# A new head and new plan values for a fused softmax-attention and linear-attention kernel

## The chip, the cores and the metric

One Trainium2 chip, one core. The metric is the device time of one execution in microseconds (us). A run's *span*, from the profiler, is about 2 us shorter than its time. Every run also reports the mean clock granted to TensorE (1.00 is full speed).

## The reference

Two attention branches work on the same x (2048 tokens, width 512, 32 heads of 16) and are mixed by a gate.

```python
g = sigmoid((x * gate_w).sum(-1, keepdims=True))
a = softmax(q k^T / 4) v  -> heads joined -> @ A_wo        # branch A, q, k, v = x @ A_wqkv
b = phi(q) (phi(k)^T v) / (phi(q) sum(phi(k)))  -> @ B_wo  # branch B, phi = [softmax(u), softmax(-u)], u = q @ w_phi
out = g * a + (1 - g) * b
```

The expensive part is branch A: 32 heads x 2048 x 2048 scores need an exponential each.

## The kernel before

The kernel is a generator. Python code declares operations (engine, assumed duration, dependencies, priority), a list scheduler simulates the five engines once, and each engine's instructions are then emitted in the order that the simulation found. On the chip the order is fixed; semaphores only make an engine wait. Tables of numbers ("plan values") steer the scheduler.

```python
GROUPS = (3, 2)          # score tiles per exponential, in turn
LEAD = [16.455..., ...]  # when work is released, against its deadline
PACE = [2.41..., 0.458...]
OFF, PRI, SHY, FILL, SLIP, POLY, SHAPE = ...   # 33 numbers each: one per block of heads
DVE_COUNT = (1, 3, 2, ...)   # key tiles per block whose exponential VectorE computes (sum 79)
```

Branch A works in 32 blocks of 16 key tiles x 4 head pairs. Most score tiles (1732 of 128 x 512) go TensorE -> PSUM ring of 5 banks -> ScalarE exponential -> a ring of 15 SBUF slots (`ET`) -> TensorE product with V. The other 316 score tiles get their exponential from a polynomial on VectorE and GpSimd (`EW`, `Ef`, `Em`, `ED`). Branch B and the output projection fill the gaps. TensorE also runs matmuls with zeros (dummies) to keep its clock up.

The head, as it was (cut):

```python
# loads: x tiles on SyncE, three weight slices on ScalarE's queue
self.d_xr = [dma("sp", ... xr[:, t, :] <- x tile t ...) for t in range(4)]
self.d_wq = [dma("act", wpart(0, P), ...)]
self.d_wk = [dma("act", wpart(D, P), ...)]
self.d_wv = [dma("act", wpart(2 * D, P), ...)]

# transposes of x on TensorE; a dummy (ps_ring <- iden, zero) ahead and after each tile
for k in range(WARM + 5):                 # WARM = 3
    if k < WARM or k > WARM:
        ... dummy matmul 128x512 ...
    t = k - WARM
    if 0 <= t < 4:
        ... 4 transposes of x tile t; after tiles 1 and 3 copies to xT ...

# Q of 512 tokens: project, cast to qst, four masked copies qT[:, n, i] = qst * par[:, n, i]
# K of 512 tokens: project, one ScalarE copy to kT; then the first score matmuls
self.o_kT[(cp, j)] = s.op("act", 0.47, ... kT[:, cp, 0:QCH] <- bank ...)
```

An exponential waits for its scores, and for the `ET` slots it overwrites, which the product with V must have read:

```python
deps = [o_qk]
if ub - NSLOT >= 0:
    deps.append(self.o_pv[(ub - NSLOT) // 4])
```

The softmax here doesn't subtract the row's maximum and nothing guards it: scores larger than these inputs give would overflow.

## Time and profile before

| | before |
|---|---|
| time | 835.79 us (3 runs, 835.7 to 837.38) |
| span of the profiled run | 833.6 us |
| first exponential starts | 10.76 us |
| stream of exponentials | 10.76 to 826.06 us: 815.30 us |
| tail after the last exponential | 7.53 us |

The page of the kernel before: busy time by engine, then the chain of work that ended last, by engine and by line, then the costliest group (busy us, mean ns | idle just before).

```profile
PE 765.5 (92%) x5815; PEld 226.2 (27%) x5898; DVE 792.3 (95%) x1157; ACT 819.4 (98%) x765; POOL 298.1 (36%) x399
...
ACT 96%; PE 2%; DVE 1%; DMA 0%; SPq 0%; issue 0%
ACT ET L867 92%; ACT phi L1121 4%; PE ps_ring L849 1%; DMA xr<-in_A_x_dram 0%; DVE EW L952 0%; PE ps_ring L1189 0%; PE ps_mp L1189 0%; PE ps_ot L895 0%; PE ps_mp L709 0%; SPq L626 0%; DVE wphi L1049 0%; PE ps_ot L983 0%; ACT outz L1230 0%; ACT kT L756 0%; ACT xT L693 0%
...
L867 ACT ACTIVATE ET<-ps_ring 128x1536 bf16<-128x1536 f32 (+1 forms) x693 | 791.2, 1340 | 1.3 <-PE ps_ring L849 0.9
```

ScalarE (ACT) is busy 98% of the span, and 96% of the chain is ScalarE. VectorE and TensorE are nearly as busy, so they have little slack.

A record's duration includes more than ScalarE's throughput: neighbouring records overlap. The Trainium skill, "Perfetto Trace Analysis", section "DVE / Act Engine Instruction (TENSOR_ADD, Activation, etc)", explains it: a record ends when the write is acknowledged, while the next instruction may start its prefetch when the previous one has finished executing. The trace agrees: here are the two shapes of the exponential (groups by shape; after the first bar the busy time in us and the mean duration in ns).

```profile
L867 ACT ACTIVATE ET<-ps_ring 128x1536 bf16<-128x1536 f32 x346 | 537.5, 1554 | 1.3 <-PE ps_ring L849 0.9 <-PE ps_ot L895 0.3
L867 ACT ACTIVATE ET<-ps_ring 128x1024 bf16<-128x1024 f32 x347 | 391.0, 1127 | 0.0
```

The records last 1.554 and 1.127 us, but the medians of the distance from one end to the next are 1.343 and 0.917 us (0.490 us for a `phi` activation). I use those three distances throughout: what a distance exceeds them by is called a **wait in the stream**, also where the profile shows no idle engine. Summed over the stream before, these waits are 0.82 us (0.44 us at 759 us, 0.31 us between 69 and 75 us). 346 x 1.343 + 347 x 0.917 + 64 x 0.490 + 0.2 (two small activations of the gate) = 814.5 us is the floor of this stream.

The head of the kernel before (timeline: start us, duration us, engine, line, operation, count, and in brackets the idle time before it and what ended it):

```profile
0.73 1.58 ACTq L620 DMA_DIRECT2D WA<-in_A_wqkv_dram  x3
...
0.74 1.81 SPq L626 DMA_DIRECT2D xr<-in_A_x_dram  x4
...
1.53 1.46 PE L674 MATMUL ps_ring<-zero,iden 128*128 128x512 bf16 x3 [1.53 <-POOL iden L656]
...
6.22 0.28 PE L681 MATMUL ps_mp<-iden,xr 128*128 128x128 bf16 x2 [0.37 <-DMA xr<-in_A_x_dram]
...
6.66 0.60 ACT L693 ACTIVATE xT<-ps_ring 128x512 bf16<-128x512 bf16 x1 [3.03 <-PE ps_ring L681]
...
7.31 1.90 PE L709 MATMUL ps_mp<-xT,WA 128*128 128x512 bf16 x8 [0.47 <-ACT xT L693]
8.38 0.69 DVE L726 CAST qst<-ps_mp 128x512 bf16<-128x512 f32 x1 [1.30 <-PE ps_mp L709]
9.11 1.14 DVE L730 TENSOR_SCALAR qT<-qst,par 128x512 bf16<-128x512 bf16 x4
...
9.25 0.60 ACT L756 ACTIVATE kT<-ps_mp 128x512 bf16<-128x512 f32 x1 [1.99 <-PE ps_mp L709]
...
10.76 2.37 ACT L867 ACTIVATE ET<-ps_ring 128x1536 bf16<-128x1536 f32 x2 [0.91 <-PE ps_ring L849]
```

The reader sees the path: x tiles issued by SyncE, the last one landed at 6.18 us (chain of waits), its transposes at 6.22, the copy to `xT` at 6.66, projections of Q and K from 7.31, the cast of Q at 8.38, masked copies at 9.11, the copy of K at 9.25, the first exponential at 10.76.

The end of ScalarE's timeline, before: the last exponential ends at 759.44 + 66.62 = 826.06 us.

```profile
759.44 66.62 ACT L867 ACTIVATE ET<-ps_ring 128x1536 bf16<-128x1536 f32 x59 [0.33 <-PE ps_ot L895]
829.02 1.27 ACT L1230 ACTIVATE outz<-ps_mp,gcol 128x512 bf16<-128x512 f32 x2 [2.96 <-PE ps_mp L1189]
```

### The profile page before, as it was taken

To read this page: it belongs to the slowest core of one execution; us is meant where nothing else is said; L and a number is where in the kernel's file an instruction comes from. 1 tells how busy PE (TensorE), PEld (TensorE's weight loads), DVE (VectorE), ACT (ScalarE), POOL (GpSimd) and SP (SyncE) were. 2 spreads that over 40 slices of the span, in tenths; PEclk is the share of its full clock that TensorE was granted. 3 is DMA by queue.
4 is the path that set the end of the run, shared out by engine and by line. 5 is a ranking of instruction groups with operands and counts; after the bars stand their busy time and mean duration, and the time that the engine had idled before them with its cause. 6 is when DMAs were issued, how large, how long until landed. Compare 5 with 4: busy or idle time off the path is not lost.

```text
span 833.6 us, 14440 instructions
## 1 busy us (share of the span) xinstructions
PE 765.5 (92%) x5815; PEld 226.2 (27%) x5898; DVE 792.3 (95%) x1157; ACT 819.4 (98%) x765; POOL 298.1 (36%) x399
## 2 busy tenths in 40 slices
PE   8899999999999999898989999989998999889998
PEld 3223333232232322222222222222222222222222
DVE  4999999999989999999999999999999999999886
ACT  6999999999999999999999999999999999999997
POOL 1244334132213432343422433442444434442523
PEclk9999999999999999999999999999999999999999
DMA  6230100000001010101210001010000001100001
GB/s 123 59 78 2 55 4 1 4 5 4 4 14 23 11 23 15 21 11 23 42 29 20 11 10 35 17 23 10 15 11 4 17 10 23 15 10 4 4 20 33
DMA packets 49123, 17.61 MB, mean 21 GB/s; under 512 B 41504, under 2 KB 49056, under 8 KB 49056
## 3 DMA queue, kind: packets, MB, share of 16 engines
q1 hardware_dynamic: 47472, 16.29, 8.5%
q8 instruction: 46, 0.75, 0.4%
q10 hardware_dynamic: 1584, 0.39, 0.2%
q14 instruction: 21, 0.17, 0.1%
HBM read 3.69 MB, written 2.10 MB: 7 GB/s over the span
## 4 chain that ended last, share of the span: by engine, by line
ACT 96%; PE 2%; DVE 1%; DMA 0%; SPq 0%; issue 0%
ACT ET L867 92%; ACT phi L1121 4%; PE ps_ring L849 1%; DMA xr<-in_A_x_dram 0%; DVE EW L952 0%; PE ps_ring L1189 0%; PE ps_mp L1189 0%; PE ps_ot L895 0%; PE ps_mp L709 0%; SPq L626 0%; DVE wphi L1049 0%; PE ps_ot L983 0%; ACT outz L1230 0%; ACT kT L756 0%; ACT xT L693 0%
## 5 line engine op out<-in xcount | busy, mean ns | idle before, releaser
L867 ACT ACTIVATE ET<-ps_ring 128x1536 bf16<-128x1536 f32 (+1 forms) x693 | 791.2, 1340 | 1.3 <-PE ps_ring L849 0.9
L849 PE MATMUL ps_ring<-qT,kT 64*128 64x512 bf16 x1732 | 343.6, 385 | 53.8 <-ACT ET L867 40.9
L966 POOL TENSOR_SCALAR ED<-EW 128x512 int16<-128x512 int16 (+1 forms) x306 | 211.5, 706 | 401.8 <-DVE Em L975 96.5
L952 DVE TENSOR_SCALAR EW<-ps_mp 128x512 int32<-128x512 f32 x316 | 204.8, 678 | 6.5 <-PE ps_mp L941 4.4
L895 PE MATMUL ps_ot<-ET,Vaug 128*17 128x512 bf16 x1732 | 168.3, 384 | 0.6 <-DVE T L1012 0.4
L849 PEld LDWEIGHTS ps_ring<-qT,kT 64*128 64x128 bf16 x1732 | 71.6, 93 | 270.4 <-ACT ET L867 244.2
L962 POOL TENSOR_SCALAR Ef<-EW 128x1024 f16<-128x1024 uint16 (+1 forms) x85 | 83.4, 981 | 121.4 <-DVE ED L977 30.3
L912 PE MATMUL ps_ot<-zero,iden 128*32 128x512 bf16 (+2 forms) x716 | 106.0, 378 | 0.3 <-issue 0.2
L941 PE MATMUL ps_mp<-qT,kT 64*128 64x512 bf16 (+1 forms) x285 | 102.0, 380 | 2.8 <-ACT phi L1121 0.8
L977 DVE TENSOR_TENSOR ED<-ED,Em 128x2048 uint16<-128x2048 int16 x79 | 99.6, 1261 | 5.1 <-POOL ED L966 4.8
L975 DVE TENSOR_TENSOR Em<-Ef,Em 128x2048 f16<-128x2048 f16 x79 | 97.7, 1237 | 0.5
L971 DVE TENSOR_TENSOR Em<-Ef 128x2048 f16<-128x2048 f16 x79 | 96.6, 1223 | 0.8 <-POOL Ef L962 0.5
L895 PEld LDWEIGHTS ps_ot<-ET,Vaug 128*17 128x17 bf16 x1732 | 41.0, 87 | 135.7 <-issue 125.1
L962 DVE TENSOR_SCALAR Ef<-EW 128x1024 f16<-128x1024 uint16 (+1 forms) x91 | 56.5, 630 | 0.1
L973 DVE TENSOR_SCALAR Em<-Em 128x2048 f16<-128x2048 f16 x79 | 55.8, 706 | 0.2
L912 PEld LDWEIGHTS ps_ot<-zero,iden 128*32 128x32 bf16 (+2 forms) x723 | 35.4, 95 | 24.0
L941 PEld LDWEIGHTS ps_mp<-qT,kT 64*128 64x128 bf16 (+1 forms) x316 | 29.1, 95 | 45.1 <-DVE EW L952 19.5
L1125 DVE TENSOR_REDUCE fsum<-phi 128x64 f32<-128x1024 bf16 x32 | 38.3, 1198 | 2.6 <-ACT phi L1121 2.6
L1127 DVE TENSOR_TENSOR phi<-phi,frec 128x1024 bf16<-128x1024 bf16 x32 | 39.8, 1247 | 0.1
L1121 ACT ACTIVATE phi<-ps_mp 128x512 bf16<-128x512 f32 x64 | 38.2, 710 | 0.0
L709 PE MATMUL ps_mp<-xT,WA 128*128 128x512 bf16 x118 | 35.9, 383 | 1.5 <-issue 0.9
L709 PE MATMUL ps_mp<-Wp,xT 128*128 128x512 bf16 x109 | 34.8, 384 | 1.0 <-issue 0.6
(83 smaller groups left out, 391.9 us busy)
## 6 DMA issues: line engine op xcount, KB each, us to landing
qT<-qst SPq DMA_DIRECT2D x120, 16.0 KB, 1.8
out_dram<-outt SPq DMA_DIRECT2D x12, 128.0 KB, 1.7
WA<-in_A_wqkv_dram SPq DMA_DIRECT2D x3, 384.0 KB, 4.8
xr<-in_A_x_dram SPq DMA_DIRECT2D x4, 128.0 KB, 3.1
WBV<-in_B_wqkv_dram SPq DMA_DIRECT2D x1, 512.0 KB, 3.9
WoA<-in_A_wo_dram SPq DMA_DIRECT2D x1, 512.0 KB, 3.7
WoB<-in_B_wo_dram SPq DMA_DIRECT2D x1, 512.0 KB, 4.5
out_dram<-outz SPq DMA_DIRECT2D x4, 128.0 KB, 1.7
```

The lines of the kernel that those rows point to most:

```text
L849: return lambda e: e.matmul(self.ps_ring[:, x % RING, :], self.kT[r, g // 2, kt * P:(kt + 1) * P], self.qT[r, n % 2, i, :], start=True, st ...
L867: self.o_exp.append(s.op("act", w * 0.434 + 0.045, lambda e, b0=b0, s0=s0, w=w: e.activation(self.ET[:, s0:s0 + w, :], self.ps_ring[:, b0: ...
L895: return lambda e: e.matmul(self.ps_ot[32 * i:32 * i + VSL, :], self.Vaug[:, kt, h, :], self.ET[:, (4 * p + k) % NSLOT, :], start=(kt == 0 ...
L912: return lambda e: e.matmul(self.ps_ot[c:c + nc, :], self.iden[r:r + nr, 0:nc], self.zero[r:r + nr, :], start=False, stop=False, tile_posi ...
L941: return lambda e: e.matmul(self.bk(b), self.kT[r, cp, kt * P:(kt + 1) * P], self.qT[r, n % 2, i, :], start=True, stop=True, tile_position ...
L952: ws.append(s.op("dve", 0.605, lambda e, i=i, b=b: e.tensor_scalar(self.EW[:, ew.idx, i * QCH:(i + 1) * QCH], self.bk(b), float(EC), float ...
L962: fs = [s.op("pool", U * 8.26e-4 + 0.28, lambda e, c=c: e.tensor_scalar(self.Ef[:, ef.idx, U * c:U * c + U], half(0, dt.uint16, c, U), flo ...
L966: hs = [s.op("pool", W * 8.26e-4 + 0.165, lambda e, c=c: e.tensor_scalar(self.ED[:, ed.idx, W * c:W * c + W].bitcast(dt.int16), half(1, dt ...
L971: u = s.op("dve", 1.13, lambda e: e.tensor_tensor(self.Em[:], Ef(), Ef(), ALU.mult), fs + [self.ed_prev], pr, frees=[ef], port=True)
L975: g_ = s.op("dve", 1.13, lambda e: e.tensor_tensor(self.Em[:], Ef(), self.Em[:], ALU.mult), [q], pr, frees=[ef], port=True)
L977: vs = [s.op("dve", 1.13, lambda e: e.tensor_tensor(out(), out().bitcast(dt.int16), self.Em[:], ALU.add), [g_] + hs, pr, port=True)]
L1121: ex.append(s.op("act", 0.478, lambda e, sg=sg: e.activation(self.phi[:, ph.idx, :, sg, :], self.bk(b).rearrange("p (h f) -> p h f", f=DH) ...
```

## The change

Its intent: start the exponentials earlier (x tiles on two queues with weights behind them; fewer dummies; only 128 tokens of K ahead of the first scores, the other 384 into a spare PSUM bank) and fit the plan values to it.

```diff
-GROUPS = (3, 2)
+GROUPS = (2, 3)
-WARM = 3
+WARM = 4
-PACE = [2.413586301706786, 0.45802931388055307]
+PACE = [0.8933644759852923, 0.45802931388055307]
 ... new numbers in LEAD, BOUNDS, RULES, OFF, PRI, SHY, FILL, SLIP, POLY, SHAPE; DVE_COUNT moves one tile (cut) ...
-        self.d_xr = [dma("sp", ... ) for t in range(4)]
-        self.d_wq = [dma("act", wpart(0, P), 2 * P * D * 2, 0.5)]
+        self.d_xr = [dma("act" if t % 2 else "sp", ... , P * D * 2, 0.45) for t in range(4)]
+        self.d_wq = [dma("sp", wpart(0, P), 2 * P * D * 2, 0.5)]
-            if k < WARM or k > WARM:
+            if k < WARM or k == WARM + 4:
     ... Q projection, cast and masked copies get earlier priorities (cut) ...
+    def first_kT(self, dl):
+        b, m = self.proj(... xT[:, c, 0:P], P, ...)                  # K of 128 tokens
+        self.o_kT[(0, 0)] = s.op("act", 0.2, ... kT[:, 0, 0:P] <- bank ...)
+        for c in range(4):                                            # K of the other 384
+            m = s.op("pe", ... ps_ring[:, RING - 1, 0:n] <- WA, xT[:, c, P:QCH] ...)
+        self.o_k0 = s.op("dve", self.c_v(n), ... kT[:, 0, P:QCH] <- ps_ring[:, RING - 1, 0:n] ..., [m], -57)
+    def k_dep(self, n, kt):
+        return self.o_k0 if cp == 0 and 0 < kt < 4 else self.o_kT[(cp, kt // 4)]
```

## The prediction

> **What bounds the kernel now.** ScalarE. The page shows it busy 819.4 us of a span of 833.6 us; the chain of waits gives it 96%, 92% on the exponentials of the attention scores. ScalarE's timeline has three parts:
>
> - Head: the first exponential starts at 10.76 us.
> - Stream: to 826.06 us. There are 346 exponentials of three score tiles and 347 of two. Their median end-to-end distances in the trace are 1.343 and 0.917 us; 64 branch-B activations add 0.490 us each. 346 x 1.343 + 347 x 0.917 + 64 x 0.490 + 0.2 = 814.5 us, so the stream's 815.3 us hold only about 0.8 us of waiting (0.44 us at 759 us, 0.31 us between 69 and 75 us).
> - Tail: 826.06 to 833.6 us (normalise, last output matmuls, three copies, store).
>
> The change leaves the stream's work alone: the tile counts of the VectorE exponential only move one from one block to another (sum 79 as before), and (2,3) instead of (3,2) gives the same 693 exponentials. So the many plan values can win at most 0.8 us plus some tail. The rest must come from the head.
>
> **The head now** (timeline, first 13 us). The four x tiles are issued one after another by SyncE (0.43 us each); the fourth takes 4.06 us from issue and lands at 6.18. Meanwhile three weight slices from ScalarE's queue share the DMA engines: 1024-byte packets take 46 ns and 256-byte ones 17 ns, so x costs 1.5 us of 16 engines and the weights 1.6 us, interleaved from 2.0 to 5.7 us. This agrees with the Trainium skill, "DMA: Bandwidth & Descriptors", section "Issuing engines are not separate DMA queues": copies of all issuers run interleaved on the same 16 engines. Then: transposes; copies 6.66 to 7.26; projections of Q and K from 7.31; Q cast at 8.38 (0.69 us); masked Q copies (0.28 us each); K copy 9.25 to 9.85; a V projection slips in; scores at 10.18; exponential at 10.76, that is 3.45 us after the projections start.
>
> **After.** x goes first on both queues, the weights behind it. Estimate: last x lands about 4.6, projections start about 5.7 (-1.6 us). After that the Q path is the limit: 1.07 + 0.69 + 2 x 0.28 + two score matmuls 0.4 gives the exponential 2.8 us after the projections start (-0.6), near 8.5 us. K of 128 tokens is ready long before. But the second exponential needs the remaining K (384 columns, copy about 0.55 us) and the other two Q copies: a new wait of about 0.4 us. Dropping the dummies between transposes removes PE time that x used to hide (0.4 to 0.6 us each); the clock should be warm by 5.7, since in the trace dummies shrink from 0.63 to 0.41 us about 3.9 us after PE's start. The skill ("TensorE: Matmul & The Clock Gate", "What's actually happening") says about 3.4 us of sustained activity, from a free-running window, so this may vary.
>
> **Sum.** Head -1.9 (net), plan values -0.2, tail -0.3 (output sums released 3 us earlier; now seven matmuls of the last tile run after the normalisation): 835.8 -> 833.4 us, range 832.3 to 834.9. Faster by over 2%: 1%; within 2%: 98%; slower: 1%.
>
> **What would show it.** First exponential at 8.2 to 9.0 us; last x landing 4.3 to 5.0; a gap of 0.2 to 0.6 us before the second exponential; stream still 815 to 816 us with the same two distances; tail 7.0 to 7.6 us.
>
> **What would make it wrong.** Weights landing later than x (they are issued last), holding the projections; a cold PE clock in the projections (+0.9 us for Q alone); a new plan that loses more than 1 us in the stream through late scores or full buffers; or my assumption that ScalarE's rate is fixed being false.

## The result

| | before | change |
|---|---|---|
| time, median of 6 runs | 835.75 us (835.67 to 837.38) | 832.98 us (832.74 to 833.37) |
| span of the profiled run | 833.59 | 831.37 |
| first exponential | 10.76 | 9.34 |
| second exponential, after the first | 1.35 (no wait) | 1.20 (0.28 of it wait) |
| waits in the stream | 0.82 | 0.34 |
| stream | 815.30 | 814.86 |
| tail | 7.53 | 7.18 |

The ratio of the fast runs is 0.9962 (95% interval 0.9949 to 0.9974). Ratios here are the mean time of one kernel's fast runs over that of the other's of the same rounds, so they are not quite the ratio of the medians.

The page of the change, the same parts as before:

```profile
PE 760.5 (91%) x5718; PEld 224.2 (27%) x5801; DVE 790.9 (95%) x1147; ACT 818.8 (98%) x765; POOL 296.4 (36%) x356
...
ACT 97%; PE 2%; DMA 1%; DVE 0%; issue 0%; SPq 0%
ACT ET L884 93%; ACT phi L1138 4%; DMA WA<-in_A_wqkv_dram 1%; PE ps_mp L1206 0%; PE ps_ring L866 0%; PE ps_ring L1206 0%; PE ps_ot L912 0%; DVE qT L730 0%; PE ps_mp L709 0%; SPq L626 0%; DVE qst L726 0%; ACT outz L1247 0%; PE ps_ot L1000 0%; DVE kT L772 0%; ACT gpos L1058 0%
...
L884 ACT ACTIVATE ET<-ps_ring 128x1024 bf16<-128x1024 f32 (+1 forms) x693 | 790.8, 1344 | 1.5 <-PE ps_ring L866 1.5
```

The same two groups by shape, and the end of ScalarE's timeline, of the change:

```profile
L884 ACT ACTIVATE ET<-ps_ring 128x1536 bf16<-128x1536 f32 x346 | 538.8, 1557 | 0.2 <-PE ps_ring L866 0.2
L884 ACT ACTIVATE ET<-ps_ring 128x1024 bf16<-128x1024 f32 x347 | 392.3, 1131 | 1.3 <-PE ps_ring L866 1.3
```

```profile
753.91 70.28 ACT L884 ACTIVATE ET<-ps_ring 128x1536 bf16<-128x1536 f32 x62
826.99 1.27 ACT L1247 ACTIVATE outz<-ps_mp,gcol 128x512 bf16<-128x512 f32 x2 [2.80 <-PE ps_mp L1206]
```

Nothing about the exponentials changed: the same counts, the same medians of distance. The last one ends at 753.91 + 70.28 = 824.19 us. The head of the change (timeline):

```profile
0.73 0.89 ACTq L626 DMA_DIRECT2D xr<-in_A_x_dram  x2
...
0.74 0.90 SPq L626 DMA_DIRECT2D xr<-in_A_x_dram  x2
...
1.53 1.89 PE L674 MATMUL ps_ring<-zero,iden 128*128 128x512 bf16 x4 [1.53 <-POOL iden L656]
...
3.67 1.25 PE L681 MATMUL ps_mp<-iden,xr 128*128 128x128 bf16 x10 [0.26 <-DMA xr<-in_A_x_dram]
...
5.60 0.60 ACT L693 ACTIVATE xT<-ps_ring 128x512 bf16<-128x512 bf16 x1 [1.61 <-PE ps_ring L681]
...
6.44 1.25 PE L709 MATMUL ps_mp<-xT,WA 128*128 128x512 bf16 x8 [0.50 <-DMA WA<-in_A_wqkv_dram]
...
7.50 0.69 DVE L726 CAST qst<-ps_mp 128x512 bf16<-128x512 f32 x1 [1.48 <-PE ps_mp L709]
...
8.76 0.55 DVE L772 CAST kT<-ps_ring 128x384 bf16<-128x384 f32 x1
...
9.34 1.02 ACT L884 ACTIVATE ET<-ps_ring 128x1024 bf16<-128x1024 f32 x1 [1.33 <-PE ps_ring L866]
...
10.53 3.71 ACT L884 ACTIVATE ET<-ps_ring 128x1536 bf16<-128x1536 f32 x3 [0.17 <-PE ps_ring L866]
```

x has landed by 4.23 us instead of 6.18. The copy to `xT` ends at 6.20, but the projections start at 6.44, "idle until DMA WA": the Q weights landed at 6.35 in this trace. The K copy of 384 columns (`kT<-ps_ring`, 0.55 us) stands between the masked copies of Q, and the second exponential waits (0.17 us of idle in the bracket, 0.28 us against its usual distance).

The spans' difference of 2.22 us is the sum of 1.42 (first exponential) + 0.45 (stream) + 0.35 (tail). In the stream, 0.76 us of old waits went and 0.28 us came. The medians of all runs differ by more, 2.77 us; the profiled run of the change is its second slowest of six.

### The profile page after: what moved, and what is told of

Read it like the earlier page. It is cut to its first block, busy times and chain, and to the rows that moved or that the text cites. A ratio compares the mean times of both kernels' runs of the same rounds, so it can differ in the third digit from the quotient of the medians.

```text
span 831.4 us, 14203 instructions
## 1 busy us (share of the span) xinstructions
PE 760.5 (91%) x5718; PEld 224.2 (27%) x5801; DVE 790.9 (95%) x1147; ACT 818.8 (98%) x765; POOL 296.4 (36%) x356
## 4 chain that ended last, share of the span: by engine, by line
ACT 97%; PE 2%; DMA 1%; DVE 0%; issue 0%; SPq 0%
ACT ET L884 93%; ACT phi L1138 4%; DMA WA<-in_A_wqkv_dram 1%; PE ps_mp L1206 0%; PE ps_ring L866 0%; PE ps_ring L1206 0%; PE ps_ot L912 0%; DVE qT L730 0%; PE ps_mp L709 0%; SPq L626 0%; DVE qst L726 0%; ACT outz L1247 0%; PE ps_ot L1000 0%; DVE kT L772 0%; ACT gpos L1058 0%
## 5 line engine op out<-in xcount | busy, mean ns | idle before, releaser
L884 ACT ACTIVATE ET<-ps_ring 128x1024 bf16<-128x1024 f32 (+1 forms) x693 | 790.8, 1344 | 1.5 <-PE ps_ring L866 1.5
L983 POOL TENSOR_SCALAR ED<-EW 128x512 int16<-128x512 int16 (+1 forms) x256 | 202.1, 803 | 344.2 <-DVE Em L992 139.3
L912 PE MATMUL ps_ot<-ET,Vaug 128*17 128x512 bf16 x1732 | 168.5, 384 | 0.7 <-DVE T L1029 0.7
L979 POOL TENSOR_SCALAR Ef<-EW 128x1024 f16<-128x1024 uint16 (+1 forms) x92 | 91.1, 991 | 176.1 <-DVE Em L992 42.2
L958 PE MATMUL ps_mp<-qT,kT 64*128 64x512 bf16 (+1 forms) x288 | 104.7, 381 | 2.3 <-DVE EW L969 1.0
L929 PE MATMUL ps_ot<-zero,iden 128*32 128x512 bf16 (+2 forms) x618 | 99.1, 378 | 0.4 <-issue 0.3
L988 DVE TENSOR_TENSOR Em<-Ef 128x2048 f16<-128x2048 f16 x79 | 99.0, 1253 | 0.1
L912 PEld LDWEIGHTS ps_ot<-ET,Vaug 128*17 128x17 bf16 x1732 | 41.0, 87 | 139.5 <-issue 130.9
L979 DVE TENSOR_SCALAR Ef<-EW 128x1024 f16<-128x1024 uint16 (+1 forms) x80 | 53.5, 673 | 0.1
L929 PEld LDWEIGHTS ps_ot<-zero,iden 128*32 128x32 bf16 (+2 forms) x624 | 32.6, 95 | 21.8
L709 PE MATMUL ps_mp<-xT,WA 128*128 128x512 bf16 (+1 forms) x112 | 33.6, 377 | 1.2 <-DMA WA<-in_A_wqkv_dram 0.5
```

The source lines that it names most:

```text
L884: self.o_exp.append(s.op("act", w * 0.434 + 0.045, lambda e, b0=b0, s0=s0, w=w: e.activation(self.ET[:, s0:s0 + w, :], self.ps_ring[:, b0: ...
L912: return lambda e: e.matmul(self.ps_ot[32 * i:32 * i + VSL, :], self.Vaug[:, kt, h, :], self.ET[:, (4 * p + k) % NSLOT, :], start=(kt == 0 ...
L929: return lambda e: e.matmul(self.ps_ot[c:c + nc, :], self.iden[r:r + nr, 0:nc], self.zero[r:r + nr, :], start=False, stop=False, tile_posi ...
L958: return lambda e: e.matmul(self.bk(b), self.kT[r, cp, kt * P:(kt + 1) * P], self.qT[r, n % 2, i, :], start=True, stop=True, tile_position ...
L979: fs = [s.op("pool", U * 8.26e-4 + 0.28, lambda e, c=c: e.tensor_scalar(self.Ef[:, ef.idx, U * c:U * c + U], half(0, dt.uint16, c, U), flo ...
L983: hs = [s.op("pool", W * 8.26e-4 + 0.165, lambda e, c=c: e.tensor_scalar(self.ED[:, ed.idx, W * c:W * c + W].bitcast(dt.int16), half(1, dt ...
```

## The experiments

My theory: the gain sits in three places (head, waits in the stream, tail). Two questions were open: what each part of the head brings, and whether the plan values matter beyond that half microsecond. "Waits" in the tables are waits in the stream as defined above, from the one profiled run; "doubled" is the time at which the trace's clock record shows TensorE's clock going from half to full in the head.

| run | what it is | median us (runs) | before, same call | first exp. | waits | clock doubled |
|---|---|---|---|---|---|---|
| e1 | before + new plan values | 848.45 (5) | 835.69 | 12.59 | 12.30 | 11.47 |
| e2 | change with old plan values | 847.32 (4) | 835.69 | 9.76 | 11.93 | 4.82 |
| e3 | before + new queues | 835.92 (5) | 835.69 | 10.95 | 1.84 | not recorded |
| e8 | change, K copy to ScalarE, laid out anew | 857.34 (5) | 835.69 | 9.09 | 20.92 | 6.17 |
| f1 | the same, order kept | 834.50 (6) | 835.87 | 8.97 | 0.03 | 5.56 |
| f2 | change, old queues, order kept | 836.07 (6) | 835.87 | 12.62 | 1.40 | 12.40 |
| f3 | before, new queues and dummies, order kept | 834.89 (5) | 835.87 | 10.28 | 0.82 | 7.68 |
| f7 | change, one model figure nudged | 833.45 (6) | 835.87 | 8.63 | 0.34 | 4.47 |
| f0 | change again | 833.95 (6) | 835.77 | 9.41 | 0.35 | 6.94 |
| f4 | change, old dummies, order kept | 834.84 (5) | 835.77 | 10.71 | 0.34 | 8.06 |
| f6 | change, K not split, order kept | 833.64 (5) | 835.77 | 9.53 | 0.03 | 4.77 |
| f9 | change, Q cast split, weights in line, order kept | 834.89 (6) | 835.77 | 10.93 | 0.03 | 10.20 |

Each call (e1 to e8; f1 to f7; f0 to f9) ran on another chip. The medians of e1, e2, e8, f1, f2, f7, f0 and f9 contain runs with a granted clock below 1.00 (see the end of this part). Where they matter I give the runs at 1.00.

### e1 and e2: the plan values alone, the head alone

```diff
 # e1: the kernel before with the change's number tables, GROUPS and DVE_COUNT
 # e2: the change with the old number tables, GROUPS and DVE_COUNT
```

Expected of e1:

> Edit: the kernel before with nothing but the new plan values (the number tables, GROUPS and the VectorE tile counts); its loads, dummies and K projection stay. Theory A (the gain has three places: head, waits inside the stream of exponentials, tail): the head stays near 10.5 to 10.8 us, the stream's waits fall from 0.83 to 0.1-0.5 us, the tail from 7.5 to about 7.2 us; time 0.6 to 1.2 us below before. Theory B (the gain is the head alone, and the waits inside the stream are an accident of one trace): time within 0.3 us of before.

Expected of e2:

> Edit: the changed kernel with all the old plan values put back; the head (queues, dummies, split K) is the new one. Theory A: first exponential near 9.3 us plus about 0.2 us (three score tiles first again), stream waits 0.8 to 1.2 us, tail about 7.5 us; time 1.0 to 1.6 us below before, so 1 us or more is missing against the whole change. Theory B: time 2.2 to 2.8 us below before, as the whole change.

Both theories fell. e1 took 848.45 us and e2 847.32 us: each part by itself makes the kernel 10 to 13 us **slower** than before. (Three of e2's four runs had a granted clock of 0.996 to 0.998; the one at 1.00, the profiled one, took 845.26 us. The profiled run of e1 was at 1.00 too.) Heads and tails are not the reason (e2's first exponential starts at 9.76 us, its tail is 7.33 us; e1's head costs 1.83 us); 12 us of waits have appeared in the stream. ScalarE's waits in e2 (engine, line, waited for: us in total, times, longest us):

```profile
ACT ET L884 <- PE ps_ot L912: 8.4, 7, 2.8
```

Most exponentials that wait do so for `ps_ot` L912, the product of earlier exponentials with V: the `ET` ring is full. One case (timeline of e2):

```profile
764.35 1.21 DVE L994 TENSOR_TENSOR ED<-ED,Em 128x2048 uint16<-128x2048 int16 x1
...
765.62 0.39 PE L1000 MATMUL ps_ot<-ED,Vaug 128*17 128x512 bf16 x4
...
765.84 0.39 PE L912 MATMUL ps_ot<-ET,Vaug 128*17 128x512 bf16 x4
...
766.28 1.02 ACT L884 ACTIVATE ET<-ps_ring 128x1024 bf16<-128x1024 f32 x1 [2.79 <-PE ps_ot L912]
```

VectorE's polynomial for the block's last tile ends at 765.56. Its product (L1000) stands in TensorE's order ahead of the product (L912) that would free `ET` slots. ScalarE stood still for 2.79 us, and the order could not give way.

This stop is no surprise of the chip: it is in the plan. The kernel's Python can be run without a chip to print the scheduler's simulated times. In e2's, the same exponential waits 3.18 us, from 763.44 us on, with VectorE's result at 765.75. Over the whole stream the simulated times hold 13.8 us of gaps between ScalarE's instructions for e1, 12.9 for e2 and 21.3 for e8 (below), against 0.6 for the kernel before and 0.5 for the change. So the scheduler, given these values and this head, laid out a program that waits, and its own simulation shows it.

### e3: the queues alone

```diff
 # the kernel before, and of the diff only
+        self.d_xr = [dma("act" if t % 2 else "sp", ..., P * D * 2, 0.45) for t in range(4)]
+        self.d_wq = [dma("sp", wpart(0, P), 2 * P * D * 2, 0.5)]
```

> Edit: the kernel before with only the new order of the first loads on the two queues. Theory C1 (the queues alone bring the head's gain, through the earlier landing of x): x landed at 4.2-4.3 us instead of 6.2, projections start at 6.4 us, first exponential at about 9.9 us, time about 0.9 us below before. Theory C2 (the queues bring little without the other steps, because the dummies between the transposes, 0.43 us each at the cold clock, now stand on the path and the weights land late): projections start at 6.9 to 7.3 us, first exponential 10.3 to 10.8 us, time within 0.5 us of before.

C2 holds: 835.92 us against 835.69. x landed at 4.45 us, but with a dummy of 0.43 us after each tile the transposes went on to 6.6 us, and the projections started at 7.50 us, later than before (7.31). 1.84 us of waits in the stream say that the layout shifted a little too.

### e8 and f1: one move, laid out anew and in the kept order

```diff
-        self.o_k0 = s.op("dve", self.c_v(n), lambda e: e.tensor_copy(
-            self.kT[:, 0, P:QCH], self.ps_ring[:, RING - 1, 0:n]), [m], -57)
+        self.o_k0 = s.op("act", 0.4, lambda e: e.activation(
+            self.kT[:, 0, P:QCH], self.ps_ring[:, RING - 1, 0:n], ACT.Copy), [m], -1)
```

> Edit: the changed kernel with the copy of the remaining 384 columns of K moved from VectorE (0.55 us, in front of the last two masked Q copies) to ScalarE, which is idle there. Theory A (that copy makes the new wait before the second exponential): first exponential stays at 9.3 us, the second follows without a wait (0.92 us end to end, instead of 0.28 us more), time 0.2 to 0.4 us below the change. Rival (the score matmuls and the two masked Q copies alone need that time, or ScalarE's copy delays the first exponential): the second exponential still at 10.5 us or later, time unchanged.

The head did what theory A said: first exponential at 9.09, the second 0.92 us later. The kernel took 857.34 us, all runs at a granted clock of 0.990 to 0.996; the profiled one took 853.53 us and had only two short drops of 3.41 us each. ScalarE's waits in e8:

```profile
ACT ET L884 <- PE ps_ot L912: 17.5, 11, 5.5
```

After e1, e2 and e8 the theory became: every edit ahead of the scheduler makes it lay out the whole program anew, and the plan values were picked for one layout. f1 tests this. It makes the very same move, but after the scheduler has run, so that all other instructions keep their places:

```diff
                 self.s.run()
+                self.edit(self.s.out)
+    def edit(self, out):
+        o = self.o_k0
+        o.eng = "act"
+        o.fns = [lambda e: e.activation(self.kT[:, 0, P:QCH], self.ps_ring[:, RING - 1, 0:QCH - P], ACT.Copy)]
+        out.remove(o)
+        out.insert(max(out.index(d) for d in [self.k_rest, self.o_kT[(0, 0)]]) + 1, o)
```

> Edit: the same move of the 384-column K copy from VectorE to ScalarE as in e8, but made after the scheduler has run, so that every other instruction keeps the place it has in the changed kernel. Theory A (e8's 21 us of waits in the stream came from the scheduler laying out everything anew, not from the move): stream waits at most 0.2 us, the second exponential 0.92 us after the first without a wait (at 10.0 to 10.3 us), time 0.3 to 0.6 us below the changed kernel (832.98), so about 832.5 us. Rival (the move itself disturbs the stream): several us of waits again, time over 836.

Waits in the stream: 0.03 us instead of 20.92. ScalarE's waits for its exponentials in f1, all of them:

```profile
ACT ET L893 <- PE ps_ring L875: 0.5, 1, 0.5
```

That is the first exponential alone; none waits for `ps_ot`. So the 21 us of e8 came from the new layout (whose simulated times hold 21.3 us), not from the move, which itself takes the 0.28 us wait away (second exponential 0.92 us after the first). The total is less clear: the runs at clock 1.00 were 832.96, 832.72 and 834.94 us, those of f7 on the same chip 832.72 to 833.54. The 0.3 us drowns in the head's spread, which f7 and f0 show.

### f7 and f0: the same program again

```diff
 # f7: the change, with
-        self.o_kT[(0, 0)] = s.op("act", 0.2, ...)
+        self.o_kT[(0, 0)] = s.op("act", 0.25, ...)
 # f0: the change, word for word
```

> Edit: the changed kernel, with one estimate of the scheduler's model changed: the duration that it assumes for the first K copy, 0.20 to 0.25 us. No instruction is added, removed or moved to another engine by this; only the layout that the scheduler computes from it changes. Theory A (each new layout is a draw, and the plan values were picked for one layout that has no waits): 3 to 20 us of waits in the stream, time 836 to 853 us. Rival (the values fit the new head in a broader sense, and only the mixtures of old and new were bad): time within 1 us of the changed kernel.

f7 does not test what it was meant to: the emitted instructions of all five engines came out identical to the change's. It neither supports nor refutes the layout theory, but it is a repeat of the change.

> The changed kernel once more, word for word, on the chip of the next three. It is the base for them, and a test of its spread. Expected from f7, whose program came out identical to the changed one: first exponential between 8.6 and 9.4 us according to when TensorE's clock doubles in the head, the second 1.2 us later (0.28 us of it waiting), stream 814.85 us, tail 7.17 us; 832.7 to 833.5 us where the granted clock is 1.00. If the drops of the clock in the middle of a run belong to this program and not to the chip of f7, one or two runs of six at 834 to 840 us again; if to that chip alone, none.

TensorE and ScalarE in the head of f7:

```profile
5.74 1.25 PE L709 MATMUL ps_mp<-xT,WA 128*128 128x512 bf16 x8 [0.51 <-ACT xT L693]
...
8.63 1.02 ACT L884 ACTIVATE ET<-ps_ring 128x1024 bf16<-128x1024 f32 x1 [1.33 <-PE ps_ring L866]
```

and of f0:

```profile
6.12 1.65 PE L709 MATMUL ps_mp<-xT,WA 128*128 128x512 bf16 x8 [0.26 <-ACT xT L693]
...
9.41 1.02 ACT L884 ACTIVATE ET<-ps_ring 128x1024 bf16<-128x1024 f32 x1 [1.33 <-PE ps_ring L866]
```

One program, and 0.78 us between the two first exponentials. In f7 the clock doubled at 4.47 us, in the middle of the transposes (their starts go from 107 to 56 ns apart); in f0 at 6.94 us, in the middle of the Q projection. The Trainium skill, "TensorE: Matmul & The Clock Gate", section "What's actually happening", describes this: the clock is at half until a window of about 3.4 us was busy, and the window is free-running. The traces agree: the stretches at full clock from the doubling to the drop after the last work last 826.02 us in f7, f0, f1, f3, f4, f6 and the change, which is 242.0 times the 3.4133 us of the skill's 4096 cycles (the 829.44 us of the kernel before are 243.0 times), while their starts differ. So the moment of doubling falls on a grid whose phase differs from run to run.

The phase is not all. Cut every trace with a clock record into windows of 3.41 us that end at its doubling, and count TensorE's matmul records in them, dummies included. The window just before the doubling was busy for 84 to 100%. Of the earlier windows, after which the clock stayed at half, all were busy for 82% or less, but for one of 87% (f2, 5.57 to 8.98 us). These figures fit the reading that a gap in TensorE's work in the head can cost a whole window more at half clock; no run tests it alone.

### f2, f3 and f4: queues and dummies, in kept order

```diff
 # f2: the change; after the scheduler has run:
+        for t in (1, 3):
+            self.d_xr[t].eng = "sp"
+        self.d_wq[0].eng = "act"
 # f3: the kernel before; after the scheduler has run: tiles 1 and 3 to "act", the Q weights to "sp" behind
 #     tile 2, the dummies after tiles 0 to 2 taken out, one of them put ahead of the transposes
 # f4: the change; after the scheduler has run: one of the four dummies ahead taken out, a dummy after
 #     each of tiles 0 to 2 put in
```

> Edit: the changed kernel, with the first loads on their old queues (four x tiles on SyncE, all three weight slices on ScalarE), set after the scheduler has run; every engine's order of other work stays. Theory A (an order of instructions tolerates a later start; the queues' worth is the difference of the starts): last x lands near 6.2 us, projections start at 7.2 to 7.4, first exponential at 10.0 to 10.4, stream waits at most 0.5 us, time 0.6 to 1.1 us above the changed kernel. Rival (the tuned order fits only this start): 2 us or more of new stream waits.

> Edit: the kernel before, with the new queues of the first loads and the dummies as in the change (four ahead, none between the transposes), set after the scheduler has run; old plan, old whole K projection. Theory A: projections start at 6.4 to 6.6 us, first exponential at 9.7 to 10.1 (0.87 us earlier than before), stream waits 0.8 us as before, tail 7.5: time 0.6 to 1.1 us below before. Rival (queues and dummies bring nothing without split K, or the shift disturbs the old plan): time within 0.3 us of before, or above it.

> Edit: the changed kernel with three dummies back between the transposes (three ahead, one after each x tile), set after the scheduler has run. Theory A (once x lands by 4.3 us, dummies stand on the path): the copies of x start 0.8 to 1.3 us later, first exponential at 9.6 to 10.4 us, time 0.7 to 1.3 us above the change. Rival (the dummies still hide behind the loads, as in the kernel before): within 0.2 us of the change.

f3: 834.89 us, 0.98 below before (0.49 between the two profiled runs), as theory A said, with waits (0.82 us) and tail (7.50) as before. Its first exponential (10.28 us) is later than forecast although its projections started at 6.04 us; its clock doubled only at 7.68 us, during the Q projection.

f4: 834.84 us against 833.57 (median of f0's three runs at clock 1.00): the dummies cost 1.27 us here (1.0 by the spans), at the top of the forecast range. Its projections start at 7.58 us, 1.46 later than f0's.

f2: the size was wrong. Its four runs at clock 1.00 have spans of 833.3 to 834.1 us, those of f7 on the same chip 830.7 to 831.4: the old queues cost 2.6 us, not 0.6 to 1.1. TensorE and ScalarE in f2's head:

```profile
5.71 0.39 PE L687 MATMUL ps_mp<-iden,xr 128*128 128x128 bf16 x2 [1.01 <-DMA xr<-in_A_x_dram]
...
7.65 2.31 PE L715 MATMUL ps_mp<-xT,WA 128*128 128x512 bf16 x8 [0.26 <-ACT xT L699]
...
12.62 1.02 ACT L890 ACTIVATE ET<-ps_ring 128x1024 bf16<-128x1024 f32 x1 [2.35 <-PE ps_ring L872]
```

The transposes wait 1.01 us for the third x tile, the clock doubles only at 12.40 us, and the whole head runs at half clock. (The window from 2.16 us was busy for 67%.) Its first exponential starts 3.99 us after f7's: 1.91 us had passed by the start of the projections, the other 2.08 us is the same work at half clock. The kernel before has the same loads but three dummies in those gaps; its clock doubled at 5.49 us. That the missing dummies caused the late doubling fits these windows, but f2 has one profile, and f4 and f9 doubled late with the new queues. In the times, queues and dummies belong together: new queues with old dummies gain nothing on the old kernel (e3), new dummies with old queues are no faster than the kernel before (f2, 835.9 against 835.87), both gain 1.0 us (f3).

The old kernel seems to have a late doubling now and then, too: 7 of its 37 runs took 837.3 to 837.6 us, 1.8 us above most, and e1, with the same loads and dummies, was profiled with the doubling at 11.47 us and the first exponential 1.83 us later than the old kernel's. No profile caught the old kernel itself in that state, so this link is argued, not shown.

### f6: K not split

```diff
 # the change; after the scheduler has run: the four 128-column K matmuls take 512 columns, ScalarE copies 512,
 # the 384-column matmuls and VectorE's copy are taken out
```

> Edit: the changed kernel with K of all 512 tokens projected and copied at once by ScalarE, as in the kernel before; set after the scheduler has run. Theory A (the Q path sets the first exponential, so the split gains next to nothing and its second copy makes the wait): the first exponential starts 2.9 to 3.1 us after the projections (2.9 in the change), the second 0.92 to 1.0 us after the first (1.2 in the change), time within 0.3 us of the change. Rival (the split is a main part of the gain): first exponential at least 0.4 us later after the projections, time 0.4 us or more above the change.

```profile
5.88 1.04 PE L722 MATMUL ps_mp<-xT,WA 128*128 128x512 bf16 x4 [0.47 <-ACT xT L706]
...
7.82 0.60 ACT L493 ACTIVATE kT<-ps_mp 128x512 bf16<-128x512 f32 x1 [1.99 <-PE ps_mp L490]
...
8.56 0.61 PE L722 MATMUL ps_mp<-WA,xT 128*128 128x128 bf16 x8 [0.78 <-ACT kT L493]
...
9.53 4.62 ACT L899 ACTIVATE ET<-ps_ring 128x1024 bf16<-128x1024 f32 x4 [1.12 <-PE ps_ring L881]
```

Theory A was wrong for the first exponential: it starts 3.65 us after the projections (9.53 - 5.88) instead of 2.89 in f7, both with the clock already at full. The lines show why. In TensorE's kept order a V projection (8.56) stands ahead of the scores, and it waits 0.78 us for the copy of K, which holds its PSUM bank. It was right for the second: no wait, 0.92 us after the first. The second starts 4.57 us after the projections against 4.09 in f7. So within this order the split is worth 0.48 us at the second exponential, and 0.3 us less than at the first. The medians (833.64 against 833.57 for f0 at clock 1.00) don't resolve that; f6's profiled run had an early doubling.

### f9: a try at a better head

```diff
 # the change; after the scheduler has run: f1's move; the Q projection in two halves of 256 tokens, in two PSUM
 # banks, cast by VectorE and ScalarE at the same time; Q, K and V weights in that order on SyncE's queue
```

> Edit: the changed kernel with three things more, set after the scheduler has run: the 384-column K copy on ScalarE (as f1), the Q projection in two halves of 256 tokens in two PSUM banks, one cast by VectorE and one by ScalarE at the same time, and the three weight slices one behind the other on SyncE's queue in the order Q, K, V. Theory A (what now limits the head is the cast of Q, 0.69 us, and its two masked copies): first exponential 2.3 to 2.6 us after the projections instead of 2.9, the second without a wait, stream 814.5 us; time 0.4 to 0.9 us below the change's repeat in runs at full clock. Rival (something else holds the scores): first exponential still 2.9 us after the projections, time unchanged.

It did not pay. The second exponential has no wait, and the Q weights landed at 5.04 us, but the projections started at 6.33, no earlier than in the change (5.74 to 6.44), for they still need the copies of x. The clock doubled only at 10.20 us in the profiled run, so the first exponential came 4.6 us after the projections. The runs at clock 1.00 were 834.74, 833.01 and 835.03 us. That is no better than the change. Whether the different spacing of TensorE's work makes a late doubling more likely, one trace cannot say. No version here is shown to beat the change.

### Runs with a dropped clock

The 31 runs of the kernel before in these calls all had a granted clock of 1.00, and so had the change's first six. But f0 and f7, which are the change, had 5 of 12 runs below: 834.25, 835.61 and 835.71 us at 0.998, 839.59 and 839.79 us at 0.989. f1, f2 and f9, with the same order in the stream, had 8 of 18. f4 and f6 have that order too and had 0 of 10, e3 and f3, with the old plan's order, 0 of 10. f2's profile caught one drop: stretches of 3.4 us ahead of it and in it (length, busy us of PE, PEld, DVE, ACT and POOL, granted clock, DMA share, GB/s).

```profile
732.60:736.00 3.40, 2.35 (x17) 0.77 (x16) 3.40 (x7) 3.40 (x4) 1.67 (x2) 1.00 0.02 6
736.00:739.40 3.40, 3.29 (x18) 0.45 (x16) 2.38 (x4) 3.23 (x3) 1.82 (x3) 0.50 0.31 39
```

The record shows half clock from 736.02 us for 3.41 us, one window, and 1.37 us of f2's 1.40 us of waits follow in it or right behind it. TensorE was not idle before: 2.35 us of 3.40. I found no threshold of activity that separates this from windows in which the clock stayed up (e1 kept full clock after a window busy for 58%, from 567.84 us; f2 lost it after 69%), so the cause stays open. What is shown is the cost: in the two later calls the change lost part or all of its gain in 5 of 12 runs. With them, the 95% intervals of the ratio, 0.9958 to 1.0003 (f7) and 0.9963 to 1.0007 (f0), include 1, though every run of the change at clock 1.00 (832.72 to 833.64 us) is faster than every run of the kernel before beside it (835.44 us and more).

## Why the prediction was right, and where it was not

The time was right: 832.98 us measured, 833.4 forecast, range 832.3 to 834.9. The sum held while its terms missed in opposite directions: in the profiled runs the head gave 0.76 us less than forecast and the plan values 0.56 us more. That these cancelled is luck.

- **The bound.** Right. ScalarE's stream is the floor; the distances 1.343 and 0.917 us are the same before and after, and the gain came from the ends and from the few waits.
- **Head, -1.9 us net.** The mechanism was right, the size not for the profiled run: -1.42 + 0.28 = -1.14 us. The first exponential, forecast for 8.2 to 9.0, came at 9.34; f7 gave 8.63 and a net gain of 1.85, f0 9.41. The terms that moved: when the clock doubles (4.47 us in f7, 5.77 in the profiled change, 6.94 in f0; I had put it at "warm by 5.7") and when the Q weights land (5.47, 6.35 and 6.03 us in the same three, and only in the profiled change did the projections wait for them; one of the risks that I named). x landed at 4.23 us, just below my 4.3 to 5.0. (A small slip: the trace's 256-byte packets take 18 ns, not 17, so the weights cost 1.7 us of the DMA engines.) The new wait before the second exponential, forecast 0.4, was 0.28 us and its cause as named: f1 removes it by moving the K copy.
- **Dummies.** Forecast: 0.4 to 0.6 us of TensorE time each that x used to hide. f4 put three back: 1.27 us for all three, 0.42 each. The link between dummies, queues and the clock (f2) I had not seen.
- **Plan values, -0.2 us.** Mis-sized. The stream lost 0.76 us of old waits (0.82 to 0.06 us, without the new wait). My bound of 0.8 us was right, but I read it as "these values hardly matter". With the new head and the old values the kernel takes 847.3 us (e2; 845.3 at full clock). With this head, the values are what keeps the stream without waits.
- **Tail, -0.3 us.** Measured -0.35. No run tests its reason: the layouts of e1, e2, e3 and e8, two of them with the old values, also have tails of 7.13 to 7.33 us.
- **Not foreseen:** the drops of the clock, in 5 of the 12 later runs of the change.

What stays open: which window of TensorE's activity lets the clock drop, and why the scheduler, with values that fit one head, lays out 13 to 21 us of gaps for another. One stretch of e2 shows how such a gap looks (a late VectorE result ahead of an urgent product in a fixed order), not which value makes it.

## What to carry to other kernels

When an engine's stream is already saturated, read the gain of a change off its ends and off the few waits inside, and check with the distances between instruction ends, not with busy time. In a kernel whose instruction order is computed, test a part by editing the order after the scheduler has run: e8 and f1 made the same move and differ by 20.9 us of waits. Look at the scheduler's simulated times first, which cost no chip: they end at 833.16 us for the kernel before and at 831.05 for the change, 2.11 us apart where the profiled spans differ by 2.22, and they hold the gaps of e1, e2 and e8. And in the first ten microseconds look at the clock before the instructions: the same program started its stream 0.8 us apart according to when TensorE's clock doubled.

## What the Trainium skill lacked or had wrong

- "TensorE: Matmul & The Clock Gate", "What's actually happening", advises not to fit the ramp to a cold count because its penalty is below 1% of a typical span. True here (0.8 us of 831 between f7 and f0), but a change of 2.8 us can be undone by it: with the doubling at 12.40 us (f2) the first exponential starts 4.97 us after the projections, with the doubling at 4.47 us (f7) 2.89 us after them.
- The same page, "HAM oscillation — how this bites in real kernels", ties a drop of the clock to TensorE idle gaps of more than about 3.4 us. In f2 the clock fell for 3.41 us at 736.02 us although TensorE was busy 2.35 of the 3.40 us before. The page also tells of drops under frequent short pauses, without a figure; no page gives the activity below which the clock falls.
- "DMA: Bandwidth & Descriptors", "Issuing engines are not separate DMA queues", says that issuing from several engines only saves issue time, usually small. It was not small here: with x on two queues ahead of the weights the last x tile was issued at 1.19 us instead of 2.11 and landed at 4.23 instead of 6.18, with the same bytes, so issue time is 0.92 of the 1.95 us. The rest came with the weights behind x (the last of the three slices landed at 7.15 instead of 6.40); no run separates the two.
- No page has the cost of a fixed instruction order whose computed layout holds gaps: 11.9 to 20.9 us of waits in a stream of 815 us (e1, e2, e8).
